# Expert rows loaded after the previous buffer's last reader, 64-bit weights turned in two parts, GpSimd's subtractions cut into pieces

## The chip, the cores and the metric

The kernel runs on one core of a Trainium2 chip. A core has TensorE (PE in the profile; its weight loads are PEld), VectorE (DVE), ScalarE (ACT), GpSimd (POOL) and SyncE (SP, which here only starts transfers). The metric is the device time of one execution in microseconds (us). Three executions of the kernel before took 1007.85, 1008.3 and 1010.31 us; the median is 1008.3 us.

## The reference

Three stages follow each other: a recurrent attention (delta rule) over 4 batches, 8 heads and 768 steps; a mixture of 8 experts in which each of 3072 tokens goes to one expert; and a gated layer with matrices of 384x1536, 384x1536 and 1536x384. Of the last two:

```python
def _moe_ref(x, w_gate, w_output_gate, w1, w2):
    logits = x @ w_gate
    e_idx = np.argmax(logits, axis=1)
    ...                                     # gate_w: softmax weight; eom: sigmoid(x @ w_output_gate)
    for e in range(E):                      # 8 experts
        mask = e_idx == e
        h = np.maximum(x[mask] @ w1[e], 0.0)
        ye = h @ w2[e]
        out[mask] = gate_w[mask, None] * eom[mask, e, None] * ye

def _moe2_ref(x, w_gate, w_val, w_out):
    gate = 1.0 / (1.0 + np.exp(-(x @ w_gate)))
    return (gate * (x @ w_val) @ w_out).astype(np.float32)
```

The matrices of the gated layer are float64; the kernel gets their bits as pairs of 32-bit words.

## The kernel before

The program has one stretch for each stage. The attention fills the first 270 us, the experts lie at about 270 to 540 us, the gated layer at 540 to 1007 us. The change touches the expert stretch.

**Precision.** Each product of float32 matrices is made of three TensorE passes, of a high and a low half: `hi` is a rounded copy (ScalarE, `copy`), `lo = src - hi` a subtraction (VectorE or GpSimd).

**Jobs and blocks.** `Experts.run` goes through nine jobs: jobs 0 and 1 are the first expert in two parts of 256 tokens, jobs 2 to 8 the other experts in windows of 460, 436, 416, 404, 396, 388 and 380 tokens. The window is in every shape (`hl 128x436` is job 3), so rows can be placed by it. A job has four blocks `j`, a block two halves `f`. In a half TensorE makes nine products of layer 1 into a PSUM tile `h` (L992, two buffers); ScalarE makes `hh = relu(h)` (L995) and VectorE `hl = max(h,0) - hh` (L996); then come nine products of layer 2 of the half before, into three tiles `y` (L955), of which three read `hl`. In block 2, `x_prep` (L903) prepares the next job: ScalarE scales its rows `XR` (L885), TensorE turns them in three groups of four (L897) into the tiles `xp`, `XTP` and a tile `h`, which takes one turn of the two `h` buffers; ScalarE and VectorE make `xh` and `xl` of them (L900, L901).

**Rows.** `rows(k)` (L873) moves a job's token rows from DRAM into `XR` (two buffers). It stands at the start of block 1 of the job before (L980). When a job's last layer-2 products are done, four small products `nm` (L968) take the token numbers out of its `XR`, ScalarE copies them into the tile (L970), and SyncE writes them out (`perm`, L971): that is the buffer's last reader.

**Expert weights.** `load` (L908) moves `w1r` and `w2r` (two buffers each), `high` makes `w1h`, `w2h` on ScalarE (L928), `low` makes `w1l`, `w2l` in one instruction of 128x768 (L933), five of sixteen on VectorE, the others on GpSimd.

**64-bit weights.** While the experts run, `hook` turns 24 tiles (128x384) of the gated layer's matrices into float32: in the second half of block `q` (from the ninth block on) it starts the load of tile `q` into one of four buffers `XG` (L828) and calls `narrow` on tile `q - 1`, five VectorE instructions (L839 to L843; below n1 to n5) that work in `XG` and in one buffer `xt`. Then ScalarE makes the high half (`wgh` or `wvh`, L815) and GpSimd the low half (`wgl` or `wvl`, L816, one instruction of 128x384). The next tile's n1 writes `xt`, so it waits for GpSimd.

**Order.** A scheduler of the framework places each engine's instructions by a model of their times; the order of the code is its starting point. So the code says what depends on what, and the built program says what stands behind what: `nm`, for one, needs only the rows, and is put where the scheduler expects them to have landed, a job early. Each engine takes its instructions strictly in that order, SyncE's transfers too. Line L78 is a wrapper, under which the instructions of the first jobs appear.

Of the kernel before, what the change touches and what calls it, by code (L numbers as in the profile page):

```python
# [7 lines left out]
F32 = mybir.dt.float32  # L8
# [5 lines left out]
ALU = mybir.AluOpType  # L14
# [798 lines left out]
def split_hi_lo(nc, hi, lo, src, eng, act=None):  # L813

    (act or nc.scalar).copy(out=hi, in_=src)  # L815
    eng.tensor_tensor(out=lo, in0=src, in1=hi, op=ALU.subtract)  # L816
# [12 lines left out]
    return r.rearrange("p (a b t) -> p a b t", a=shape[0], t=2)  # L829


def narrow(nc, t, r):

    if r.dtype == F32:
        return r
    V = nc.vector
    u = t.bitcast(U32)
    lo, hi = r[..., 0], r[..., 1]
    V.tensor_scalar(out=u, in0=hi, scalar1=3, scalar2=0x3FFFFFFF, op0=ALU.logical_shift_left, op1=ALU.bitwise_and)  # L839
    V.scalar_tensor_tensor(out=u, in0=hi, scalar=0xC0000000, in1=u, op0=ALU.bitwise_and, op1=ALU.bitwise_or)  # L840
    V.tensor_scalar(out=hi, in0=u, scalar1=0xFF800000, scalar2=None, op0=ALU.bitwise_and)
    V.scalar_tensor_tensor(out=lo.bitcast(F32), in0=lo, scalar=2.0**-52, in1=hi.bitcast(F32), op0=ALU.mult, op1=ALU.mult)
    V.tensor_tensor(out=t, in0=lo.bitcast(F32), in1=t, op=ALU.add)  # L843
    return t


# [10 lines left out]
class Experts:  # L857
# [72 lines left out]

    def low(self, b, i, engine):
        h, l = self.W[b][i]
        engine.tensor_tensor(out=l, in0=self.raw[b][i], in1=h, op=ALU.subtract)  # L933

    def split(self, upto):
        while self.n_split < min(upto, len(self.blocks)):
# [8 lines left out]
    def run(self, y2T, pp, xp, hook=lambda q, f: None, first=False):  # L945
        sp, jobs = self.sp, self.jobs
        self.xp = [(pp, "xp", 1), (xp, "XTP", 1), (pp, "h", 2)]
        own, b, pend = {}, -1, None

        def layer2(p):  # L950
            k, f, w2, hh, hl, ys = p
            n = jobs[k].n
            for c in range(3):
                for i, (l, r) in enumerate(PASS):
                    self.T.matmul(out=ys[c][:, 0:n], lhsT=w2[l][:, f % 2, 128 * c : 128 * c + 128], rhs=(hh, hl)[r], start=(f == 0 and i == 0), stop=(f == 7 and i == 2), skip_group_check=True)  # L955
            if f == 7:
                off = jobs[k].off
                for c in range(3):
                    o = y2T[:, c, ds(off, n)]
                    if c == 1:  # L960
                        self.A.copy(out=o, in_=ys[c][:, 0:n])
                    else:
                        self.V.tensor_copy(out=o, in_=ys[c][:, 0:n])

                ps = xp.tile([128, 512], F32, tag="GL", name="nm", bufs=1)[0:1].rearrange("p (r q) -> p r q", r=4)[:, :, 0 : n // 4]
                XR = self.XR.pop(k)
                for r in range(4):
                    self.T.matmul(out=ps[:, r], lhsT=XR[0 : n // 4, r, 384:385], rhs=self.idt[0 : n // 4, 0 : n // 4], start=True, stop=True)  # L968
                row = XR[0:1].rearrange("p r c -> p (r c)")[:, 0:n]
                self.A.copy(out=row.rearrange("p (q r) -> p q r", r=4), in_=ps.rearrange("p r q -> p q r"))  # L970
                self.SP.dma_start(out=self.perm[ds(off, n)].rearrange("n o -> o n"), in_=row)  # L971

        for q in range(4 * len(jobs)):
            k, j = divmod(q, 4)
            job = jobs[k]
            n = job.n
            if j == 0:
                ys = [pp.tile([128, 512], F32, tag=f"y{c}", name=f"y{c}") for c in range(3)]
            if j == 1 and k + 1 < len(jobs) and not first:
                self.rows(k + 1)  # L980
            if not job.shares:
                b += 1
                own[j] = b
                if not first:
                    self.load(b + 3)
            w1, w2 = self.W[own[j]]
            xh, xl = self.X[k]
            for f in (2 * j, 2 * j + 1):
                hp = pp.tile([128, 512], F32, tag="h", name="h", bufs=2)
                for i, (l, r) in enumerate(PASS):  # L990
                    for c in range(3):
                        self.T.matmul(out=hp[:, 0:n], lhsT=w1[l][:, c, 128 * (f % 2) : 128 * (f % 2) + 128], rhs=(xh, xl)[r][:, c], start=(i == 0 and c == 0), stop=(i == 2 and c == 2))  # L992
                hh = sp.tile([128, WMAX], F32R, tag="hh", name="hh", bufs=2)[:, 0:n]
                hl = sp.tile([128, WMAX], F32R, tag="hl", name="hl", bufs=2)[:, 0:n]
                self.A.activation(out=hh, in_=hp[:, 0:n], func=AF.Relu)  # L995
                self.V.scalar_tensor_tensor(out=hl, in0=hp[:, 0:n], scalar=0.0, in1=hh, op0=ALU.max, op1=ALU.subtract)  # L996
                if f % 2 == 0 and not first:
                    self.split(b + 2)
                if pend:
                    layer2(pend)  # L1000
                pend = (k, f, w2, hh, hl, ys)
                hook(q, f % 2)
                first = first and q < 7
            if j == 2 and k + 1 < len(jobs) and not first:
                self.x_prep(k + 1, self.A)
        layer2(pend)


def kernel_body(tc, a, out):
    nc = tc.nc  # L1010
    V, A, G, T, SP = nc.vector, nc.scalar, nc.gpsimd, nc.tensor, nc.sync
    with ExitStack() as ctx:
# [11 lines left out]
        if True:  # L1024
# [13 lines left out]
            gs = ctx.enter_context(tc.tile_pool(name="gt_s", bufs=1, side="left"))  # L1038
            jobs = [Job(E0), Job(E1, row=E0, shares=True)] + [Job(n) for n in WINS]
# [40 lines left out]
            gv = [[yp.tile([128, 3, DF2], F32R, name=n + p) for p in "hl"] for n in ("wg", "wv")]  # L1080
# [44 lines left out]
            wide = {}  # L1125
# [1 line left out]
            keep = [t.rearrange("p c f -> p (c f)") for t in gv[1]]  # L1127
            E.keep = {2: keep[0], 3: keep[1]}
            E.n_split = 2
            queued, head = [], []  # L1130

            def first_high():

# [3 lines left out]
            def hook(q, f):  # L1137
                i = 2 * q + f
                if i == 0:
                    E.high(2)  # L1140
                    E.low(2, 0, E.G)
                    tail(1)
                elif i == 1:
                    tail(2)
                    tail(3)
                    E.low(2, 1, E.V)
                elif i == 2:
                    E.high(3)
                    E.low(3, 0, E.V)
                    E.low(3, 1, E.V)  # L1150
                    E.n_split = 4
                elif i == 3:
                    order()
                    E.rows(1)
                    E.load(6)
                if i == QX:
                    E.x_scale(1, (E.V, E.A))
                if i == QT:
                    for c in range(3):
                        E.x_turn(1, c)  # L1160
                if i in (10, 12):
                    E.split(E.n_split + 1)
                if i == 14:
                    queued.append(E.SP)
                    nc_ = tc.nc
                    E.use((nc_.vector, nc_.scalar, nc_.gpsimd, nc_.tensor, nc_.sync))
                if i == 10:
                    E.rows(2)
                if i == QS:
                    E.x_scale(2, (E.V,))  # L1170
                if i == 13:
                    for c in range(3):
                        E.x_turn(2, c)
                if i == SG:
                    A.activation(out=key[:, 0:1], in_=cst[0:1, 0:1], func=AF.Sigmoid)
                if i == YS:
                    head.extend(gs.tile([128, 2, ROW], F32, tag="XG", name="XG", bufs=4).rearrange("p a b -> p (a b)")[:, 0:512].bitcast(F32R) for _ in range(3))
                    first_high()
                if f == 0 or q < 8:
                    return  # L1180
                q -= 8
                if q < 24:
                    r = gs.tile([128, 2, ROW], F32, tag="XG", name="XG", bufs=4).rearrange("p a b -> p (a b)")
                    wide[q] = load_wide(queued[0] if q < 4 else SP, r, gv_src(q)[2], [3, 128])
                if 1 <= q < 25:
                    w, cols, _ = gv_src(q - 1)
                    f = narrow(nc, gs.tile([128, 3, 128], F32, tag="xt", name="xt", bufs=1), wide.pop(q - 1))
                    split_hi_lo(nc, *[t[:, :, cols] for t in gv[w]], f, G)

            with tc.tile_pool(name="ex_p", bufs=1, reuse_waits="tile", space=PSUM) as pp:  # L1190
                E.run(y2T, pp, gp, hook, True)
# [4 lines left out]
            with tc.If(placed < NTOK):  # L1196
                with tc.tile_pool(name="ov", bufs=1) as ov:
                    q = ov.tile([1, 2, 64 + NE * NW_], F32, name="ov_q")
                    tab = ov.tile([1, 4, NE * NW_], I32, name="ov_tab")
                    z = ov.tile([112, ROW], F32, name="ov_z")  # L1200
                    first = ov.tile([1, NE], F32, name="ov_first")
# [191 lines left out]
```

## Time and profile before

| | |
|---|---|
| median of three runs | 1008.3 us |
| profiled execution, its own time | 1008.28 us |
| span of its instructions | 1006.6 us |
| TensorE busy, whole span | 946.6 us (94%) |
| TensorE busy, 300 to 536 us (experts) | 223.98 of 236 us |
| TensorE busy, 545.5 to 975 us (gated layer) | 429.5 of 429.5 us |
| mean granted TensorE clock | 0.905 |

Times are counted from the first instruction of the span. A row of the timeline gives start, duration, engine, line, operation, and in brackets how long the engine sat idle before it and what it then waited for. A row of the waits gives the sum, the number of times and the longest. The granted clock is a share of 2.4 GHz: 1.00 is 2.4 GHz, 0.50 is 1.2 GHz.

### The profile page before, as it was taken

The page shows a single profiled execution, that of the slowest core. Times are in us where ns is not written, and L with a number is a line of the kernel's source. Part 1 is how long each engine was busy: PE and PEld are TensorE (multiplying, and loading weights), DVE is VectorE, ACT ScalarE, POOL GpSimd, SP SyncE. Part 2 cuts the span into 40 slices and gives each one's busy share as a digit, 9 for nine tenths or more (in the row PEclk, how much of TensorE's full clock was granted, in tenths as well). Part 3 has the DMA queues.
Part 4 walks back from the last instruction along what each step waited for, and adds up shares of the span by engine and source line. Part 5 has one row for each costly group of instructions (what it writes and reads, how often), then busy time and mean ns, then how long its engine had stood idle before and what let it go on. Part 6 is the DMA issues. An engine that isn't in the chain of part 4 may idle for free. (4 is left out here: it accounts for less than half of the span.)

```text
span 1006.6 us, 24686 instructions
## 1 busy us (share of the span) xinstructions
PE 946.6 (94%) x10261; PEld 834.2 (83%) x10262; DVE 494.0 (49%) x1379; ACT 368.7 (37%) x723; POOL 346.1 (34%) x439
## 2 busy tenths in 40 slices
PE   6888879899999989989999999999999999999996
PEld 6677768778898879889897888888888888888885
DVE  6999897984458776777534644113113112111111
ACT  2654546566445444445452222112112112111111
POOL 4363254442313444345340334222222222222322
PEclk7776687675599999989999999999999999999999
DMA  5878652234346445645422220000000000000000
GB/s 123 154 226 188 143 131 57 72 94 128 102 133 204 142 144 169 200 128 151 130 85 49 63 63 27 21 1 9 24 1 9 24 1 8 24 1 8 23 1 33
DMA packets 62871, 82.90 MB, mean 82 GB/s; under 512 B 10313, under 2 KB 55634, under 8 KB 62754
## 3 DMA queue, kind: packets, MB, share of 16 engines
q1 hardware_dynamic: 59042, 70.49, 26.2%
q0 software_dynamic: 3712, 10.78, 3.1%
q8 instruction: 82, 1.34, 0.6%
q14 instruction: 35, 0.29, 0.1%
HBM read 64.13 MB, written 15.80 MB: 79 GB/s over the span
## 5 line engine op out<-in xcount | busy, mean ns | idle before, releaser
L1314 DVE TENSOR_TENSOR gf<-gf,g 128x512 f32<-128x512 f32 x72 | 49.5, 688 | 312.7 <-PE g L1306 310.2
L816 POOL TENSOR_TENSOR gsl<-gf,gsh 128x512 fp32r<-128x512 f32 x68 | 89.3, 1314 | 273.6 <-ACT gsh L815 273.6
L1313 ACT ACTIVATE gf<-g 128x512 f32<-128x512 f32 x72 | 43.0, 597 | 191.2 <-PE g L1306 191.2
L815 ACT CAST gsh<-gf 128x512 fp32r<-128x512 f32 x69 | 42.8, 620 | 145.0 <-DVE gf L1314 143.0
L1280 PE MATMUL o<-wol,gsh 128*128 128x384 f32 x272 | 87.1, 339 | 0.0
L1280 PE MATMUL o<-woh,gsl 128*128 128x384 f32 x272 | 86.6, 336 | 0.0
L78 DVE TENSOR_TENSOR tmp<-X,Lt 128x96 f32<-128x96 f32 (+40 forms) x301 | 72.4, 271 | 1.6
L78 DVE TENSOR_TENSOR X<-X,tmp 128x96 f32<-128x96 f32 (+40 forms) x301 | 71.5, 268 | 1.0
L78 PE MATMUL GY<-KQ 48*64 48x128 f32 (+1 forms) x640 | 46.3, 405 | 20.6 <-DMA KQ<-in_st_dram 13.8
L996 DVE SCALAR_TENSOR_TENSOR hl<-h,hh 128x460 fp32r<-128x460 f32 (+7 forms) x57 | 33.1, 581 | 64.2 <-ACT hh L995 63.9
L1306 PE MATMUL g<-yl,wgh 128*128 128x512 f32 x216 | 62.5, 394 | 0.0
L1306 PE MATMUL g<-yl,wvh 128*128 128x512 f32 x216 | 62.4, 395 | 0.0
L1280 PE MATMUL o<-woh,gsh 128*128 128x384 f32 x272 | 62.2, 339 | 0.0
L955 PE MATMUL y<-hh,w2h 128*128 128x460 f32 (+6 forms) x168 | 60.8, 362 | 1.3 <-ACT hh L995 1.2
L1306 PE MATMUL g<-yh,wgh 128*128 128x512 f32 x180 | 60.7, 394 | 0.0
L955 PE MATMUL y<-hh,w2l 128*128 128x460 f32 (+6 forms) x168 | 58.5, 348 | 0.0
L78 PEld LDWEIGHTS GY<-KQ 48*64 48x64 f32 x640 | 35.6, 205 | 26.1 <-issue 13.0
L1280 PEld LDWEIGHTS o<-woh,gsh 128*128 128x128 f32 x272 | 49.7, 188 | 6.2
L1280 PEld LDWEIGHTS o<-wol,gsh 128*128 128x128 f32 x272 | 50.6, 188 | 2.4
L933 POOL TENSOR_TENSOR w1l<-w1r,w1h 128x768 fp32r<-128x768 f32 x19 | 37.1, 1953 | 44.2 <-ACT w1h L928 44.0
L1306 PE MATMUL g<-yh,wgl 128*128 128x512 f32 x180 | 51.8, 394 | 0.0
L1306 PE MATMUL g<-yh,wvh 128*128 128x512 f32 x180 | 51.6, 394 | 0.0
(325 smaller groups left out, 2228.3 us busy)
## 6 DMA issues: line engine op xcount, KB each, us to landing
w1r<-in_w_dram SPq DMA_DIRECT2D x32, 384.0 KB
w2r<-in_w_dram SPq DMA_DIRECT2D x32, 384.0 KB
KQ<-in_st_dram SPq DMA_DIRECT2D x40, 192.0 KB
disp<-zrow SPq DMA_DIRECT2D x8, 772.0 KB
VT<-in_vtok_dram SPq DMA_DIRECT2D x96, 48.0 KB
kt<-in_ktok_dram SPq DMA_DIRECT2D x96, 48.0 KB
XG<-in_m2g_dram SPq DMA_DIRECT2D x12, 384.0 KB
XG<-in_m2v_dram SPq DMA_DIRECT2D x12, 384.0 KB
```

Source lines behind the costliest of these rows:

```text
L78: r = f(*args, **kw)
L815: (act or nc.scalar).copy(out=hi, in_=src)
L816: eng.tensor_tensor(out=lo, in0=src, in1=hi, op=ALU.subtract)
L933: engine.tensor_tensor(out=l, in0=self.raw[b][i], in1=h, op=ALU.subtract)
L955: self.T.matmul(out=ys[c][:, 0:n], lhsT=w2[l][:, f % 2, 128 * c : 128 * c + 128], rhs=(hh, hl)[r], start=(f == 0 and i == 0), stop=(f == 7 ...
L996: self.V.scalar_tensor_tensor(out=hl, in0=hp[:, 0:n], scalar=0.0, in1=hh, op0=ALU.max, op1=ALU.subtract)
L1280: T.matmul(out=ops_[m][:, 0:384], lhsT=gh[l][:, 128 * m : 128 * m + 128], rhs=wo[r][:, f], start=(f == 0 and i == 0), stop=(f == 11 and i ...
L1306: T.matmul(out=ps, lhsT=gv[w][l][:, c, 128 * f : 128 * f + 128], rhs=Y[r][c], start=(i == 0 and c == 0), stop=(i == 2 and c == 2))
L1313: A.activation(out=gf, in_=gps[0], func=AF.Sigmoid)
L1314: V.tensor_tensor(out=gf, in0=gf, in1=gps[1], op=ALU.mult)
```

## The change

Three edits. `rows(k + 2)` is issued right behind the `perm` transfer of job `k` instead of at block 1 of job `k + 1`. `narrow` is cut behind its third instruction: n1 to n3 are issued in a block's first half, n4, n5, the high copy and the subtraction in its second, so that an `hl` lies between. GpSimd's subtractions are issued in pieces: three of 128x256 for `w1l`, two of 128x384 for `w2l`, three of 128x128 for `wgl` and `wvl`; those of VectorE stay whole.

```diff
     def low(self, b, i, engine):
         h, l = self.W[b][i]
-        engine.tensor_tensor(out=l, in0=self.raw[b][i], in1=h, op=ALU.subtract)
+        r = self.raw[b][i]
+        if engine is self.G:
+            for k in range(r.shape[1]):
+                engine.tensor_tensor(out=l[:, k], in0=r[:, k], in1=h[:, k], op=ALU.subtract)
+        else:
+            engine.tensor_tensor(out=l, in0=r, in1=h, op=ALU.subtract)
...
                 self.SP.dma_start(out=self.perm[ds(off, n)].rearrange("n o -> o n"), in_=row)
+                if 0 < k < len(jobs) - 2:
+                    self.rows(k + 2)
...
-            if j == 1 and k + 1 < len(jobs) and not first:
-                self.rows(k + 1)
...
-                if f == 0 or q < 8:
+                if q < 8:
                     return
                 q -= 8
+                if f == 0:
+                    if 1 <= q < 25:
+                        turn.append(narrow_ops(nc, gs.tile([128, 3, 128], F32, tag="xt", name="xt", bufs=1), wide.pop(q - 1)))
+                        for op in turn[0][1][:3]:
+                            op()
+                    return
...
                     w, cols, _ = gv_src(q - 1)
-                    f = narrow(nc, gs.tile([128, 3, 128], F32, tag="xt", name="xt", bufs=1), wide.pop(q - 1))
-                    split_hi_lo(nc, *[t[:, :, cols] for t in gv[w]], f, G)
+                    f, ops = turn.pop()
+                    for op in ops[3:]:
+                        op()
+                    hi, lo = [t[:, :, cols] for t in gv[w]]
+                    A.copy(out=hi, in_=f)
+                    for c in range(3):
+                        G.tensor_tensor(out=lo[:, c], in0=f[:, c], in1=hi[:, c], op=ALU.subtract)
```

`narrow_ops` returns the five instructions of `narrow` as a list; `narrow` itself, used in the gated layer, runs them one after the other as before.

The scheduler makes its own order of this. On VectorE, around the third turn of job 3's rows (`xl<-h,xh 128x436`) in job 2; n1 is `xt<-XG` (TENSOR_SCALAR), n2 `xt<-XG,xt` (SCALAR_TENSOR_TENSOR), n3 `XG<-xt`, n4 `XG<-XG`, n5 `xt<-XG,xt` (TENSOR_TENSOR). Before:

```order
L996 SCALAR_TENSOR_TENSOR hl<-h,hh 128x460
L841 TENSOR_SCALAR XG<-xt 128x384
L842 SCALAR_TENSOR_TENSOR XG<-XG 128x384
L1119 TENSOR_LOAD tab
L843 TENSOR_TENSOR xt<-XG,xt 128x384
L901 TENSOR_TENSOR xl<-h,xh 128x436
L839 TENSOR_SCALAR xt<-XG 128x384
L840 SCALAR_TENSOR_TENSOR xt<-XG,xt 128x384
L996 SCALAR_TENSOR_TENSOR hl<-h,hh 128x460
```

Now:

```order
L1010 SCALAR_TENSOR_TENSOR hl<-h,hh 128x460
L844 TENSOR_TENSOR xt<-XG,xt 128x384
L1133 TENSOR_LOAD tab
L910 TENSOR_TENSOR xl<-h,xh 128x436
L840 TENSOR_SCALAR xt<-XG 128x384
L841 SCALAR_TENSOR_TENSOR xt<-XG,xt 128x384
L1010 SCALAR_TENSOR_TENSOR hl<-h,hh 128x460
```

n3 and n4 of the earlier tile have moved in front of the first `hl`; n1 and n2 of the next still stand in front of the second.

On SyncE, around the start of job 3 (window 436): from the `perm` transfer of that job, which the scheduler has put early, to the load of job 4's rows (`XR<-disp 112x1544`), which go into the buffer of job 2. Before:

```order
L971 DMA perm<-XR 1x436
L828 DMA XG<-in_m2v_dram 128x3x256
L916 ISA
L916 DMA w1r<-in_w_dram 128x3x256
L828 DMA XG<-in_m2g_dram 128x3x256
L917 ISA
L917 DMA w2r<-in_w_dram 128x2x384
L1116 TENSOR_LOAD tab
L876 ISA
L876 DMA XR<-disp 112x1544
```

Now:

```order
L985 DMA perm<-XR 1x436
L925 ISA
L925 DMA w1r<-in_w_dram 128x3x256
L828 DMA XG<-in_m2v_dram 128x3x256
L926 ISA
L926 DMA w2r<-in_w_dram 128x2x384
L1130 TENSOR_LOAD tab
L885 ISA
L885 DMA XR<-disp 112x1544
```

One `XG` load less stands in this piece; the rows still stand behind a `w1r`, an `XG` and a `w2r` load.

On ScalarE, in job 6 (window 396) just ahead of the copy of the token numbers `XR<-nm 1x388`. Before:

```order
L928 CAST w2h<-w2r 128x768
L815 CAST wvh<-xt 128x3x128
L995 ACTIVATE hh<-h 128x396
L928 CAST w1h<-w1r 128x768
L970 COPY XR<-nm 1x388
```

Now:

```order
L1009 ACTIVATE hh<-h 128x396
L909 CAST xh<-XTP 128x388
L937 CAST w2h<-w2r 128x768
L1009 ACTIVATE hh<-h 128x396
L937 CAST w1h<-w1r 128x768
L984 COPY XR<-nm 1x388
```

The high copy `wvh` no longer stands between `w2h` and this `hh`.

## Rows read from the trace of the kernel before

**Rows 1.** Windows: length, busy us (count) of each engine, PEclk, DMA, GB/s.

```profile
300.00:536.00 236.00, 223.98 (x1243) 207.43 (x1241) 151.99 (x238) 111.36 (x204) 99.90 (x62) 0.98 0.49 147
378.20:381.60 3.40, 3.40 (x11) 3.09 (x11) 2.15 (x5) 0.62 (x2) 0.38 (x1) 0.51 0.94 313
443.10:449.90 6.80, 5.78 (x17) 5.68 (x18) 3.68 (x8) 2.61 (x5) 1.00 (x1) 0.50 0.53 176
545.50:975.00 429.50, 429.50 (x2039) 373.14 (x2038) 99.51 (x163) 94.57 (x161) 121.04 (x100) 1.00 0.06 19
```

**Rows 2.** Waits of TensorE, 300 to 536 us: sum, times, longest.

```profile
PE h L992 <- DVE hl L996: 4.8, 2, 2.9
PE nm L968 <- DMA XR<-disp: 3.1, 2, 1.7
PE y L955 <- ACT hh L995: 1.2, 2, 1.0
PE y L955 <- DVE hl L996: 0.9, 2, 0.7
PE h L992 <- DVE xl L901: 0.8, 1, 0.8
PE h L78 <- DVE hl L78: 0.7, 1, 0.7
```

**Rows 3.** Timeline of TensorE: the three longest waits of the stretch.

```profile
358.05 0.34 PE L968 MATMUL nm<-cst,XR 104*1 104x104 f32 x2 [1.70 <-DMA XR<-disp]
...
377.52 0.66 PE L992 MATMUL h<-xh,w1h 128*128 128x436 f32 x2 [1.92 <-DVE hl L996]
...
444.12 1.38 PE L992 MATMUL h<-xh,w1h 128*128 128x404 f32 x3 [2.92 <-DVE hl L996]
```

**Rows 4.** Timeline, VectorE and ScalarE before the stall at 377 us.

```profile
371.24 0.36 DVE L839 TENSOR_SCALAR xt<-XG 128x384 uint32<-128x384 uint32 x1
...
372.38 0.54 ACT L995 ACTIVATE hh<-h 128x436 fp32r<-128x436 f32 x1 [0.97 <-PE h L992]
...
376.86 0.60 DVE L996 SCALAR_TENSOR_TENSOR hl<-h,hh 128x436 fp32r<-128x436 f32 x1
```

**Rows 5.** Timeline, VectorE and GpSimd before the stall at 444 us.

```profile
438.09 1.99 POOL L933 TENSOR_TENSOR w2l<-w2r,w2h 128x768 fp32r<-128x768 f32 x1
...
438.42 2.08 DVE L840 SCALAR_TENSOR_TENSOR xt<-XG,xt 128x384 uint32<-128x384 uint32 x1
...
440.04 2.13 POOL L933 TENSOR_TENSOR w1l<-w1r,w1h 128x768 fp32r<-128x768 f32 x1
...
440.53 1.86 DVE L841 TENSOR_SCALAR XG<-xt 128x384 uint32<-128x384 uint32 x1
...
443.50 0.57 DVE L996 SCALAR_TENSOR_TENSOR hl<-h,hh 128x404 fp32r<-128x404 f32 x1
```

**Rows 6.** Line 816, GpSimd and others: ns min/median/max, starts.

```profile
L816 POOL TENSOR_TENSOR wgl<-xt,wgh x12: 1009/1020/1664, 311.7 to 481.7; 128x384 fp32r<-128x384 f32 x12
```

**Rows 7.** Line 933, the same columns.

```profile
L933 POOL TENSOR_TENSOR w1l<-w1r,w1h x19: 1822/1852/2292, 332.0 to 525.3; 128x768 fp32r<-128x768 f32 x19
```

**Rows 8.** Timeline, VectorE and GpSimd before the wait at 347 us.

```profile
344.74 1.85 POOL L933 TENSOR_TENSOR w2l<-w2r,w2h 128x768 fp32r<-128x768 f32 x1 [0.37 <-ACT w2h L928]
344.80 2.21 DVE L840 SCALAR_TENSOR_TENSOR xt<-XG,xt 128x384 uint32<-128x384 uint32 x1
...
346.94 0.62 DVE L996 SCALAR_TENSOR_TENSOR hl<-h,hh 128x460 fp32r<-128x460 f32 x1
```

**Rows 9.** Timeline, VectorE's n5 and SyncE's transfers from 348 us.

```profile
348.46 0.56 DVE L843 TENSOR_TENSOR xt<-XG,xt 128x384 f32<-128x384 f32 x1
...
349.05 0.37 SPq L828 DMA_DIRECT2D XG<-in_m2g_dram  x1
...
350.82 0.34 SPq L876 DMA_DIRECT2D XR<-disp  x1
```

**Rows 10.** Timeline, VectorE before the wait at 311 us.

```profile
309.01 2.06 DVE L843 TENSOR_TENSOR xt<-XG,xt 128x384 f32<-128x384 f32 x1
```

More of the change, by code (lines that the diff above doesn't have):

```diff
@@ L829, in load_wide, with narrow_ops @@
     return r.rearrange("p (a b t) -> p a b t", a=shape[0], t=2)
-def narrow(nc, t, r):
+def narrow_ops(nc, t, r):
     if r.dtype == F32:
-        return r
+        return r, []
     V = nc.vector
@@ L838, in narrow @@
     lo, hi = r[..., 0], r[..., 1]
[L839 to L843, printed above, removed]
+    return t, [
+        lambda: V.tensor_scalar(out=u, in0=hi, scalar1=3, scalar2=0x3FFFFFFF, op0=ALU.logical_shift_left, op1=ALU.bitwise_and),
+        lambda: V.scalar_tensor_tensor(out=u, in0=hi, scalar=0xC0000000, in1=u, op0=ALU.bitwise_and, op1=ALU.bitwise_or),
+        lambda: V.tensor_scalar(out=hi, in0=u, scalar1=0xFF800000, scalar2=None, op0=ALU.bitwise_and),
+        lambda: V.scalar_tensor_tensor(out=lo.bitcast(F32), in0=lo, scalar=2.0**-52, in1=hi.bitcast(F32), op0=ALU.mult, op1=ALU.mult),
+        lambda: V.tensor_tensor(out=t, in0=lo.bitcast(F32), in1=t, op=ALU.add),
+    ]
+def narrow(nc, t, r):
+    t, ops = narrow_ops(nc, t, r)
+    for f in ops:
+        f()
     return t
@@ L1129, in kernel_body @@
             E.n_split = 2
-            queued, head = [], []
+            queued, head, turn = [], [], []
             def first_high():
```

## The prediction

> **What bounds the kernel now.** I read the busy time by stretch first. In the gated layer TensorE works without a gap (429.50 of 429.50 us from 545.5 us), at a granted clock of 1.00; the attention is untouched by the edits. In the expert stretch, 300 to 536 us, TensorE is busy 223.98 of 236 us, so 12.0 us are idle, and two pieces of 3.4 and 6.8 us run at 0.50 of the clock, 1.2 GHz, in which half the time is lost: 5.1 us [rows 1]. Nothing else is to be had: 17.1 us at most. What TensorE gains here reaches the end one for one, because it is the only busy engine behind it.
>
> The waits of TensorE, read next, say who holds it up: twice VectorE's `hl`, from which a PSUM buffer `h` becomes free (4.8 us, the longer 2.9); twice the landing of the next job's rows, at `nm` (3.1, longer 1.7); and five small waits on `hh`, `hl` and `xl` [rows 2]. The timeline places the long ones: rows at 358 us (1.70), `hl` at 377 (1.92) and at 444 (2.92) [rows 3]. The waits at 377 and at 444 are the two with a half-rate piece behind them (378.2 and 443.1 us), the second the longer; behind the 1.70 there is none.
>
> Why is `hl` late? At 377 its input `hh` was ready at 372.92 and `hl` began at 376.86: it stood behind n1 to n5 [rows 4]. An n3 needs 0.36 us like the n1 in that group, an n5 0.56 [rows 4, 9]. Beside GpSimd's subtractions they take about 2: at 438 us n2 took 2.08 and n3 1.86, and each ended 0.4 and 0.2 us after a GpSimd instruction [rows 5]. So VectorE's work between SBUF buffers and GpSimd's exclude each other for a whole instruction. `hl` reads PSUM and kept its 0.6 us everywhere. The two also take turns: GpSimd's second subtraction stood right behind its first (438.09 + 1.99 = 440.08), yet n2 got in between, GpSimd waited for it (2.13 instead of 1.85), and then n3 lost again [rows 5, 7].
>
> **GpSimd's pieces.** 384 elements take 1.02 us and 768 take 1.85 [rows 6, 7], so an instruction costs 0.19 us plus 2.17 ns an element: a piece of 256 is 0.74 us, of 128 0.47. `w1l` becomes 2.2 us (+0.4), `w2l` 2.0 (+0.2), the low half of a turned tile 1.4 (+0.4). GpSimd is busy 99.9 of the 236 us and has room [rows 1]; the +0.4 delays the next tile's n1, which waits for it.
>
> What a piece saves depends on how many of VectorE's instructions meet GpSimd ahead of an `hl`.
> - One meets it: at 344.80 n2 waited for a whole `w2l` and `hl` began at 346.94 [rows 8]. With pieces the first ends at 345.76, n2 0.4 later, and `hl` begins at 346.1, 0.8 earlier: the wait of 0.7 on it goes [rows 2]. −0.7.
> - At 309 us n5 met `w2l`, and an n3 had met `w1l` before it [rows 10]. A `w1l` in pieces holds n3 to n5 for three pieces of 0.74 and the `w2l` comes too late for them. The 0.7 on `hl` at L78 goes too. −0.7.
> - At 377 and at 444 all of n2 to n5 stand ahead of `hl`, in the built order after the change as before it. At 444, step by step with the overlaps of [rows 5]: piece of `w2l` to 439.11, n2 to 439.53, piece to 440.38, n3 to 440.60, piece of `w1l` to 441.17, n4 to 441.59, piece to 442.16, n5 to 442.58. Two lost turns of 1.85 have become four of 0.74 to 1.02, so `hl` comes at 442.5 instead of 443.50: 1.0 earlier. If n1 comes 0.4 later and loses a turn itself, 0.2 earlier. I take 0.6 at either place: −1.2, bounds 0 and −4.8.
>
> The Trainium skill has a rule that would give more: in "SBUF — State Buffer", section "Who interferes with whom", the instruction that issues second is blocked until the first has finished, and no more is said. Read so, VectorE would wait for one piece, once, and the long waits would be gone; the trace agrees on the lock (2.08 us for an n2) and adds that the next instruction loses again.
>
> **The turned weights.** The built order changes less than the code: the scheduler had already put `hl` between n-instructions. Three places gain. On ScalarE the `hh` in job 6 no longer stands behind the copy of a turned tile: the longer wait on `hh`, 1.0 us, goes. −1.0. The `xl` that cost 0.8 has n4 and n5 ahead of it instead of n1 to n3, of which one met GpSimd: −0.5, bounds 0 and −0.8 [rows 2]. And n3, n4 come ahead of an `hl` in job 2, so that n5 is earlier.
>
> **The rows.** Their transfer is not much earlier in the built order: one `XG` load less ahead of it in job 2, and still one with a wait. In the trace that load waited for n5 (348.46 + 0.56 = 349.02), went out at 349.05, the rows' transfer at 350.82 [rows 9], and they landed by 358.05. So the landing follows that n5, and it is the lock that moves it: with n2 0.8 earlier and n3 to n5 held by one piece, n5 ends 0.8 to 1.5 earlier. `nm` itself has moved back by three products in jobs 3 and 5, some 0.6 us (an estimate; two products show 0.66 with their overlap [rows 3]). In job 3 TensorE comes to `nm` at 356.35 − 0.7 + 0.6 = 356.25, the rows at 358.05 − 1.2 = 356.85: the wait falls from 1.7 to 0.6, −1.1. In job 5 1.4 falls to 0.1, −1.3. Together −2.4, bounds 0 (the same n5 holds it) and −3.1.
>
> **The clock.** If the wait at 377 is 1.3, it is shorter than the 1.70 that had no half-rate piece behind it; at 2.3 the one at 444 lies between those with 3.4 and with 6.8 us. I count one piece of 3.4 us less, half of it: −1.7, bounds 0 and −5.1.
>
> **What is given back.** Rows of the order in jobs 6 and 7 get n-instructions that stood elsewhere, every tile is turned 0.4 us slower, and ScalarE's copies of `nm` and `xh` stand behind others. The trace has no price for these; nearest are the small waits of 0.7 to 1.0 [rows 2]. I take two and a half of 0.7, +1.8, bounds 0 and +5.
>
> **Sum.** −0.7 − 0.7 − 1.2 − 1.0 − 0.5 − 2.4 − 1.7 + 1.8 = −6.4. The profiled execution took 1008.28 us (span 1006.6 and 1.7 around it), the median of three is 1008.3: 1001.9 us.
>
> **Rivals.**
> 1. *Slower: the turns.* VectorE loses a turn to every piece. With the low half of a tile 0.4 later, GpSimd's `w2l` gets ahead of n1, and ahead of one `hl` stand five lost turns instead of two. The place is the third turn of the rows in each job, where a `h` buffer hangs on `hl` directly (377 and 444 us). If the next narrowing is late there by 1 us or more, job 3's wait is 3.0 with 6.8 us at half rate (+1.1 + 1.7), job 5's the same +0.4, and job 4 gets what job 3 has now (1.9 + 1.7). With −1.4 from 309 and 345 us: +5.4, 1013.7 us. For it: n3 lost again right after n2 [rows 5]. Against it: the walk above, in which four short turns are less than two long ones. It decides once n1 meets a piece itself. Chance 0.12.
> 2. *No change: the waits move.* The long `hl` rows are unchanged in the order, the rows hang on the same n5, the clock falls as before; only 309, 345 us and the `hh` gain (−2.4), and new small waits give +1.8 back: 1007.7 us. For it speaks how little the order changes. Chance 0.25.
> 3. *One lost turn only.* If VectorE loses to one piece and then gets ahead, both long waits go (−4.8) with both half-rate pieces (−5.1), and the rest as above without what is given back (−5.3): −15.2, 993.1 us. Against it stands [rows 5]. This is what the rule of the Trainium skill by itself would make of it. Chance 0.13.
>
> **How the numbers follow.** The forecast has 0.50; its own range, by the bounds of the clock and of what is given back, is 997.5 to 1005. Runs of this kernel can tell 0.3%, 3 us, from no change. Faster by more: forecast and rival 3, 0.63. Within: rival 2, 0.25. Slower: rival 1, 0.12. Leaving out the far half of rival 3 and most of rival 1, the range for 8 in 10 is 995 to 1009.5.
>
> **What would show it.** n-instructions of about 1.2 us at most instead of 2; GpSimd's pieces at 0.74 and 0.47; no wait on `hl` near 311 and 347 us; `nm` waiting under 0.7; the waits on `hl` in jobs 3 and 5 (436 and 404) still there, at 1.3 and 2.3, with at most one half-rate piece of 3.4 us between 370 and 450 us. I am wrong if those two waits are gone or longer than before, or if waits on `hl`, `hh` or `xl` of over 1 us stand where there are none now.

## The result and the profile after

The changed kernel takes 998.47 us (median of four runs, 996.54 to 1000.42), the kernel before 1008.92 us (four runs, 1007.85 to 1010.31): a ratio of 0.988, 95% interval 0.985 to 0.991. Forecast were 1001.9 us and a range of 995 to 1009.5, so the time lies 3.4 us below the forecast, inside its range. The profiled execution took 996.54 us, with a span of 994.8 us against 1006.6 before.

First the place of the difference. Windows of the kernel after (columns as in [rows 1]): the whole expert stretch, from the first layer-1 product to the first product of the gated layer; the part of it that answers to [rows 1]; and the gated layer.

```profile
274.96:528.93 253.97, 248.57 (x1492) 234.34 (x1493) 159.83 (x299) 125.04 (x232) 132.31 (x179) 0.98 0.50 149
300.00:525.80 225.80, 223.45 (x1291) 210.30 (x1290) 144.34 (x241) 113.86 (x208) 124.59 (x169) 1.00 0.52 155
545.50:975.00 429.50, 429.50 (x2042) 373.37 (x2041) 92.62 (x151) 93.96 (x160) 119.73 (x99) 1.00 0.05 18
```

The same whole stretch of the kernel before:

```profile
271.44:541.96 270.52, 256.05 (x1493) 238.01 (x1493) 168.92 (x299) 123.90 (x232) 107.34 (x70) 0.97 0.47 140
```

The stretch is 16.5 us shorter with the same 299 instructions on VectorE, which is busy 9.1 us less, and with 109 instructions more on GpSimd, which is busy 25 us more. From 300 us to its end (the second line) TensorE is idle 2.35 us where it was 12.0, and no piece runs at half rate (1.00 against the 0.98 of [rows 1]). The rest of the program is longer by 4.7 us in this pair of executions: the attention, which no edit touches, by 3.5, and the gated layer, whose clock is taken up in the last section, by 1.2. So the span falls by 11.8.

Waits of TensorE in the kernel after, 290 to 540 us, where [rows 2] had six lines (the first one here is the entry into the gated layer, which is outside [rows 2]):

```profile
PE g L1331 <- PEq L1221: 3.0, 1, 3.0
PE h L1006 <- DVE hl L1010: 1.9, 2, 1.2
PE nm L982 <- DMA XR<-disp: 0.4, 1, 0.4
```

The two waits on `hl` are the ones forecast to stay, in jobs 3 and 5. They are 1.17 and 0.76 us where [rows 3] had 1.92 and 2.92; the 1.70 on the rows is gone. TensorE in the kernel after, the two places:

```profile
376.50 0.87 PE L1006 MATMUL h<-xh,w1h 128*128 128x436 f32 x3 [1.17 <-DVE hl L1010]
...
437.21 0.82 PE L1006 MATMUL h<-xh,w1h 128*128 128x404 f32 x3 [0.76 <-DVE hl L1010]
```

Timeline of VectorE and GpSimd in the kernel after, before the first of them (it answers to [rows 4]; a GpSimd row joins the pieces of one subtraction, as x2 and x3):

```profile
371.16 0.36 DVE L840 TENSOR_SCALAR xt<-XG 128x384 uint32<-128x384 uint32 x1 [0.34 <-POOL wvl L1213]
371.18 2.51 POOL L945 TENSOR_TENSOR w2l<-w2r,w2h 128x384 fp32r<-128x384 f32 x2
371.55 1.26 DVE L841 SCALAR_TENSOR_TENSOR xt<-XG,xt 128x384 uint32<-128x384 uint32 x1
372.85 1.06 DVE L842 TENSOR_SCALAR XG<-xt 128x384 uint32<-128x384 uint32 x1
373.65 2.86 POOL L945 TENSOR_TENSOR w1l<-w1r,w1h 128x256 fp32r<-128x256 f32 x3
373.94 0.97 DVE L843 SCALAR_TENSOR_TENSOR XG<-XG 128x384 f32<-128x384 uint32 x1
374.95 0.97 DVE L844 TENSOR_TENSOR xt<-XG,xt 128x384 f32<-128x384 f32 x1
375.84 0.60 DVE L1010 SCALAR_TENSOR_TENSOR hl<-h,hh 128x436 fp32r<-128x436 f32 x1
```

Each of n2 to n5 loses one turn, to a piece: 1.26, 1.06, 0.97, 0.97 us. GpSimd pays too: its five pieces take 5.37 us here, where the unblocked lengths add up to 4.3. Still n1 to n5 take 4.8 us from the start of the first to the end of the last, where it was 5.7. The lines of n2, n3 and GpSimd's pieces over the whole kernel (minimum, median, maximum in ns):

```profile
L841 DVE SCALAR_TENSOR_TENSOR xt<-XG,xt x24: 544/559/1266, 309.6 to 486.1; 128x384 uint32<-128x384 uint32 x24
L842 DVE TENSOR_SCALAR XG<-xt x24: 351/362/1069, 310.2 to 487.6; 128x384 uint32<-128x384 uint32 x24
...
L945 POOL TENSOR_TENSOR w1l<-w1r,w1h x57: 722/742/1375, 334.2 to 513.1; 128x256 fp32r<-128x256 f32 x57
L945 POOL TENSOR_TENSOR w2l<-w2r,w2h x32: 1000/1148/1436, 331.8 to 510.7; 128x384 fp32r<-128x384 f32 x32
```

A lost turn costs n2 0.7 us instead of the 1.5 of [rows 5]. The `w1l` piece takes 0.74 us, as worked out from [rows 6, 7].

### The profile page after: what moved, and what is told of

The parts are those of the page before. It is cut to its first block, busy times and chain, and to the rows that moved or that the text cites. A ratio compares the mean times of both kernels' runs of the same rounds, so it can differ in the third digit from the quotient of the medians.

```text
span 994.8 us, 24800 instructions
## 1 busy us (share of the span) xinstructions
PE 943.7 (95%) x10261; PEld 833.7 (84%) x10262; DVE 484.5 (49%) x1379; ACT 370.4 (37%) x723; POOL 374.5 (38%) x548
## 5 line engine op out<-in xcount | busy, mean ns | idle before, releaser
L945 POOL TENSOR_TENSOR w1l<-w1r,w1h 128x256 fp32r<-128x256 f32 x57 | 47.5, 860 | 32.5 <-ACT w1h L937 32.5
```

Source lines behind the costliest of these rows:

```text
L945: engine.tensor_tensor(out=l[:, k], in0=r[:, k], in1=h[:, k], op=ALU.subtract)
```

## The experiments

All ratios are to the kernel before on the same chip, with 95% intervals. "Stretch" is the expert stretch of the profiled execution, measured as above; "n time" is the sum of the 120 instructions n1 to n5 of the 24 tiles, which is 57 us where nothing blocks them; "half rate" lists the lengths in us of the pieces at a granted clock of 0.50 from 300 us on, without the one that some kernels have at the entry into the gated layer.

| kernel | ratio | stretch | n time | `hl` waits of `h` | half rate |
|---|---|---|---|---|---|
| before | 1 | 270.5 | 86.6 | 1.92, 2.92 | 3.4, 6.8 |
| after | 0.988 (0.985 to 0.991) | 254.0 | 77.2 | 1.17, 0.76 | none |
| e1 pieces only | 0.986 (0.981 to 0.991) | 256.0 | 77.0 | 1.21, 0.76 | none |
| e2 rows and two parts | 1.000 (0.997 to 1.003) | 265.2 | 86.4 | 1.93, 2.90 | none |
| e3 whole, order of after | 0.9985 (0.996 to 1.001) | 267.1 | 91.6 | 3.13, 3.07 | 3.4, 6.8 |
| e4 finer pieces | 0.987 (0.983 to 0.992) | 255.4 | 70.6 | 0.45, 0.88 | none |
| e5 weights' pieces | 0.988 (0.983 to 0.993) | 258.4 | 78.0 | 2.37 | 3.4 |
| e6 tiles' pieces | 0.995 (0.991 to 0.998) | 262.3 | 91.3 | 3.8 in all | 3.4 |
| e7 weights on VectorE | 0.986 (0.981 to 0.990) | 249.4 | 57.1 | none | none |
| e8 changed kernel again | 0.985 (0.982 to 0.989) | 255.8 | 77.7 | 1.19, 0.76 | none |
| e9 as e7, more runs | 0.984 (0.981 to 0.988) | 252.2 | 57.0 | none | none |
| e10 before, weights on VectorE | 0.986 (0.982 to 0.990) | 252.7 | 57.0 | none | none |

**Which edit does it (e1 to e3).** e1 has the pieces alone:

```diff
...
+        if engine is self.G:
+            for k in range(r.shape[1]):
+                engine.tensor_tensor(out=l[:, k], in0=r[:, k], in1=h[:, k], op=ALU.subtract)
...
-                    split_hi_lo(nc, *[t[:, :, cols] for t in gv[w]], f, G)
...
+                    A.copy(out=hi, in_=f)
+                    for c in range(3):
+                        G.tensor_tensor(out=lo[:, c], in0=f[:, c], in1=hi[:, c], op=ALU.subtract)
```

> The kernel before with GpSimd's subtractions in pieces and neither of the other two edits. Its instructions stand in the changed kernel's order on every engine. Theory L (the pieces alone) and theory O (the order that the scheduler makes when it sees pieces): both 998 us, ratio 0.988. Theory P (the moved rows and the two parts of the turning each have a share): over 1002 us.

e2 has the two other edits and whole subtractions:

```diff
-            if j == 1 and k + 1 < len(jobs) and not first:
-                self.rows(k + 1)
...
+                if 0 < k < len(jobs) - 2:
+                    self.rows(k + 2)
...
+                    f, ops = turn.pop()
+                    for op in ops[3:]:
+                        op()
                     split_hi_lo(nc, *[t[:, :, cols] for t in gv[w]], f, G)
```

> The rows' load moved and the turning in two parts, no pieces. The built order is that of the kernel before on every engine. Theories L and O: 1008.5 us, ratio 1.000 within 0.003. Theory P: 3 to 6 us faster than before.

e3 keeps the subtractions whole and adds behind each some of two elements, so that the scheduler sees as many instructions as in the changed kernel and builds very nearly the same order. The small ones write values that are there already:

```diff
         engine.tensor_tensor(out=l, in0=self.raw[b][i], in1=h, op=ALU.subtract)
+        if engine is self.G:
+            for k in range(1, self.raw[b][i].shape[1]):
+                engine.tensor_tensor(out=l[:, k, 0:2], in0=self.raw[b][i][:, k, 0:2], in1=h[:, k, 0:2], op=ALU.subtract)
...
```

> Whole subtractions on GpSimd, each followed by subtractions of 2 elements that write the same values again, as many as there are further pieces. The scheduler then makes the changed kernel's order (TensorE and ScalarE the same, VectorE but for one place, SyncE but for two). Theory L (VectorE waits for shorter instructions): the n-instructions take up to 2 us again, waits on hl of 2 us at windows 436 and 404 come back, with half-rate pieces: 1005 to 1009 us. Theory O (the order): 998 to 1000 us, no long waits.

The pieces alone give 989.28 us against 1003.29, as much as all three edits. The two code moves together give none, and the reason is in the build: with them the scheduler puts out the instructions of the kernel before, in the same order on every engine. With the pieces alone it puts out the order of the changed kernel. Every move of an instruction that the rows of the order under "The change" show was therefore the scheduler's answer to the pieces. e2's waits of TensorE (282 to 528 us) are those of [rows 2] but for the rows' landing:

```profile
PE h L1001 <- DVE hl L1005: 4.8, 2, 2.9
PE nm L977 <- DMA XR<-disp: 2.2, 2, 1.2
PE y L964 <- ACT hh L1004: 1.2, 2, 1.0
```

e3 separates the order from the length. Its waits of TensorE in the same stretch:

```profile
PE h L995 <- DVE hl L999: 6.2, 2, 3.1
PE nm L971 <- DMA XR<-disp: 1.1, 2, 0.7
PE y L958 <- DVE hl L999: 1.0, 1, 1.0
PE h L78 <- DVE hl L78: 0.7, 1, 0.7
```

The order alone removes the waits on `hh` and `xl` and shortens those on the rows, makes the two `hl` waits longer by 1.4 us and adds one of 1.0 in job 4: no gain is shown, 0.9985 (0.996 to 1.001). So the gain hangs on the length of GpSimd's instructions. The pieces in the order of the kernel before were not run; how much of the gain needs the new order beside them stays open. The half-rate pieces are there again, behind the two long waits:

```profile
375.50:378.90 3.40, 3.40 (x11) 3.10 (x10) 2.05 (x5) 1.22 (x2) 0.51 (x4) 0.50 0.90 295
440.30:447.10 6.80, 6.12 (x18) 6.04 (x19) 4.25 (x9) 2.61 (x5) 1.61 (x5) 0.50 0.54 176
```

**Which pieces, and how fine (e4 to e6).** e4 halves the pieces of the experts' weights:

```diff
+            n = r.shape[2] // 2
             for k in range(r.shape[1]):
-                engine.tensor_tensor(out=l[:, k], in0=r[:, k], in1=h[:, k], op=ALU.subtract)
+                for s in (slice(0, n), slice(n, 2 * n)):
+                    engine.tensor_tensor(out=l[:, k, s], in0=r[:, k, s], in1=h[:, k, s], op=ALU.subtract)
```

> The changed kernel with w1l in six pieces of 128x128 and w2l in four of 128x192. Theory L: n-instructions beside w1l and w2l take 0.8 to 1.0 us at most, the waits of 1.17 and 0.76 us at windows 436 and 404 shrink to under 0.6, 997 to 999 us (little is left to gain). Rival (the turns: a lost turn for every piece, so more pieces cost more): hl comes later than in the changed kernel, waits over 1.2 us, 1001 us or more. The order changes too, which blurs it.

e5 has, of e1's two hunks, only the first (`w1l`, `w2l`), e6 only the second (`wgl`, `wvl`).

> The kernel before with pieces for w1l and w2l alone; wgl and wvl stay one instruction of 128x384. Theory L: the long lost turns are those beside w1l and w2l, so nearly all of the gain stays: ratio 0.986 to 0.991, waits on hl at windows 436 and 404 of 0.7 to 1.3 us. Rival (the turned tiles' low half, released earlier piece by piece, matters): ratio over 0.994.

> Pieces for wgl and wvl alone; w1l and w2l stay whole. Theory L: n-instructions still up to 2 us, waits on hl of 2 to 3 us, ratio 0.996 to 1.003. Rival as in the run before: ratio under 0.992.

e4's n2 line, which answers to the L841 line above:

```profile
L841 DVE SCALAR_TENSOR_TENSOR xt<-XG,xt x24: 541/558/983, 305.4 to 484.3; 128x384 uint32<-128x384 uint32 x24
```

More turns at half the length cost no more: n time falls by another 6.6 us, and GpSimd's is up by 20 us over the stretch with nobody waiting for it. The total does not show it (990.56 us beside e1's 989.28), since only some 2 us of waits were left. Of the two waits that were to shrink to under 0.6 us one did (0.45); the other is 0.88. The weights' pieces alone bring the gain (0.988, overlapping e1's interval), but not as expected in the trace: one wait on `hl` is gone and the other, at window 404, is 2.37 us instead of 0.7 to 1.3. e6 missed its expectation: the tiles' pieces leave n time above that of before, 91.3 us, and still gain 0.2 to 0.9%. That n time does not fall has a reason in the program: n1 waits for the earlier tile's subtraction, so n1 to n5 never lie beside one. Its order is another again, and its profile has one half-rate piece where before has two; the cause of that half per cent was not separated.

**The lock taken away (e7 to e10).** In e7 VectorE makes every `w1l` and `w2l`, so that GpSimd has none of them:

```diff
-                self.low(b, i, self.V if self.nw % 16 in DV else self.G)
+                self.low(b, i, self.V)
...
-                    E.low(2, 0, E.G)
+                    E.low(2, 0, E.V)
```

> The changed kernel with every w1l and w2l made on VectorE (0.95 us each, whole), so that GpSimd has only the turned tiles' pieces and nothing long is left to wait for. Theory L: every n-instruction under 1 us; VectorE's busy time rises by about 35 x 0.95 = 33 us of 236 (152 to 185), and what its load costs is seen apart from the lock: the waits on hl at windows 436 and 404 under 0.8 us. If load on VectorE counted for more than the lock, waits on hl grow and the ratio is over 0.99; else 0.985 to 0.988.

e8 is the changed kernel, e9 is e7, and e10 has e7's diff on the kernel before, without any of the three edits; all on one chip.

> The changed kernel once more, as the measure for the next two on the same chip: ratio 0.985 to 0.990.

> The kernel of e7. Its expert stretch was 249.4 us against 254.0 of the changed kernel, so by theory L it should be some 4 us faster than e8: ratio to before lower than that of e8 by 0.003 to 0.005. If VectorE's load costs elsewhere (the start of the gated layer), equal to e8.

> The kernel before with one thing changed: w1l and w2l all on VectorE; wgl and wvl whole on GpSimd (1.02 us). Theory L: what is left to wait for is 1.02 us at most, so nearly as e9, waits on hl under 0.7 us, ratio within 0.003 of e9. Rival (pieces matter for another reason than their length): ratio over 0.99.

n2 in e10, all 24 of them:

```profile
L840 DVE SCALAR_TENSOR_TENSOR xt<-XG,xt x24: 542/551/565, 308.7 to 464.5; 128x384 uint32<-128x384 uint32 x24
```

Its slowest takes 565 ns. A whole `w1l`, now on VectorE, in the same kernel:

```profile
L933 DVE TENSOR_TENSOR w1l<-w1r,w1h x26: 941/951/960, 327.0 to 509.3; 128x768 fp32r<-128x768 f32 x26
```

The n-instructions take 57.0 us together, so none is blocked any more, where the kernel before has an n2 of up to 2.2 us. This is the most direct evidence for the lock: neither instruction nor data of n2 changed, and what went is GpSimd's work beside it. (The tiles' subtractions stay on GpSimd, but n1 waits for them.) VectorE takes 0.95 us for a subtraction that costs GpSimd 1.85 [rows 7]. e10's whole stretch:

```profile
273.64:526.30 252.66, 247.66 (x1493) 235.55 (x1493) 172.02 (x338) 124.64 (x232) 36.31 (x31) 0.98 0.49 150
```

39 instructions have gone from GpSimd (70 to 31) to VectorE (299 to 338), at 0.95 us some 37 us of work, and VectorE's busy time is up by only 3.1 (168.92 to 172.02). Most of the work came back as n time, which is 29.6 lower; the two do not add up exactly, since busy time counts instructions that overlap once. The 33 us that were expected of e7 did not come either: VectorE is busy 172.85 us in its stretch, 13.0 more than in that of after.

The stretches of e9 and e10 are 3.6 and 3.2 us shorter than that of e8, but the medians are 989.31 (e8), 988.42 (e9) and 990.25 (e10) with overlapping intervals: the three cannot be told apart, and no version is shown to beat the changed kernel. e9 was expected 0.003 to 0.005 below e8 and came 0.001 below it; in the profiles the attention took 3.6 us more in e9, and the gated layer 463.1 us in both, so the load on VectorE cost nothing there. Two changed lines (e10) do as well as the three edits.

## Why the prediction was right, step by step

**The mechanism held.** GpSimd and VectorE's work between SBUF buffers exclude each other for a whole instruction, and VectorE loses again at each next instruction. The walk of four short turns instead of two long ones is what the timeline shows, also in job 5 (1.27, 1.06, 0.98, 0.97 us for n2 to n5). The sign came out, and that the two `hl` waits stay; the longest n-instruction is 1.36 us (n4) where about 1.2 was told.

**Its terms, by the rows of after and of the runs.**

- `hl` in job 2 (−0.7) and at 311 us (−0.7): both waits are gone. At 311 us it came as told: n3 to n5 stand beside the three pieces of `w1l` (0.73, 0.98 and 0.98 us). At 347 us the number is luck. n2 was to lose one short turn, and it meets no piece at all, because ScalarE makes `w2h` behind the `hh` there now: GpSimd's `w2l` starts at 347.26 us, after the `hl` at 346.32. e3, with whole subtractions in this order, has no wait there either: this 0.7 belongs to the order.
- `hl` in jobs 3 and 5 (−0.6 each): −0.75 and −2.16. From n1 to the late `hl` it took 5.62 and 5.48 us and takes 4.68 and 4.70, so the turns give 0.9 and 0.8, near the forecast's 0.6 and the walk's 1.0. The rest of job 5's was not in the sum, and is shown below.
- The rows (−2.4): 3.1 us have become 0.4, −2.7. In other executions of the same order 1.3 (e8) and, in e1, 2.1 us were left, and e2, with the order of the kernel before, has 2.2 instead of 3.1, so the size of this term is that of one pair. Its cause is in doubt too: the lock was to move the landing, and e3, with whole subtractions, has 1.1.
- `hh` (−1.0) and `xl` (−0.5): −1.2 and −0.8, both lines gone.
- The clock (−1.7): −5.1, the upper bound. Both half-rate pieces went, one was counted. The reason that was given, a wait shorter than one without such a piece, does not hold in other runs (the last section), so this term was a guess.
- Given back (+1.8): nothing. The waits of after have no line that [rows 2] lacks; only the one at the entry into the gated layer, outside [rows 2], grew from 2.45 to 3.05. The step that failed is this one, together with the clock: the sum took 0.1 us for the two (−1.7 + 1.8), and they brought −5.1.

The rest of job 5's wait comes from the tile before. VectorE, ScalarE and GpSimd in the kernel before, ahead of [rows 5], put together from the timelines of the three engines:

```profile
432.80 2.00 DVE L841 TENSOR_SCALAR XG<-xt 128x384 uint32<-128x384 uint32 x1
...
435.78 0.56 DVE L843 TENSOR_TENSOR xt<-XG,xt 128x384 f32<-128x384 f32 x1
...
437.32 0.58 DVE L996 SCALAR_TENSOR_TENSOR hl<-h,hh 128x404 fp32r<-128x404 f32 x1 [0.99 <-ACT hh L995]
...
436.37 0.51 ACT L815 CAST wgh<-xt 128x384 fp32r<-128x384 f32 x1 [4.10 <-DVE xt L843]
436.79 0.50 ACT L995 ACTIVATE hh<-h 128x404 fp32r<-128x404 f32 x1
...
436.96 1.02 POOL L816 TENSOR_TENSOR wgl<-xt,wgh 128x384 fp32r<-128x384 f32 x1 [2.39 <-ACT wgh L815]
...
438.02 0.36 DVE L839 TENSOR_SCALAR xt<-XG 128x384 uint32<-128x384 uint32 x1
```

The same place in the kernel after:

```profile
427.02 0.90 DVE L842 TENSOR_SCALAR XG<-xt 128x384 uint32<-128x384 uint32 x1
...
429.33 0.60 DVE L844 TENSOR_TENSOR xt<-XG,xt 128x384 f32<-128x384 f32 x1
...
430.93 0.58 DVE L1010 SCALAR_TENSOR_TENSOR hl<-h,hh 128x404 fp32r<-128x404 f32 x1 [0.99 <-ACT hh L1009]
...
429.97 0.52 ACT L1211 CAST wvh<-xt 128x384 fp32r<-128x384 f32 x1 [2.79 <-DVE xt L844]
430.39 0.50 ACT L1009 ACTIVATE hh<-h 128x404 fp32r<-128x404 f32 x1
...
430.56 1.29 POOL L1213 TENSOR_TENSOR wvl<-xt,wvh 128x128 fp32r<-128x128 f32 x3 [1.04 <-ACT wvh L1211]
...
431.89 0.36 DVE L840 TENSOR_SCALAR xt<-XG 128x384 uint32<-128x384 uint32 x1 [0.39 <-POOL wvl L1213]
```

In both, a blocked n3 delays n5, n5 the high copy on ScalarE, the copy GpSimd's low half, and the low half the next n1, which writes `xt`: one chain through three engines. (The `hl` ahead of n1 ends sooner, at 437.90 and 431.51.) TensorE wanted the buffer at 441.20 in the kernel before (444.12 − 2.92) and at 436.45 after (437.21 − 0.76). Counted back from there, n1 began 3.18 us ahead before and 4.56 after, 1.4 earlier. The n3 took 2.00 us in the one and 0.90 in the other, 1.1 less, and began 1.0 earlier by the same count (8.40 and 9.43 us ahead), for a reason that was not traced; of these 2.1 us, 0.4 went to the instructions between n3 and n5, where an `xl` stands now, and 0.3 to the way from n5 to n1, where the low half in pieces takes longer. I had walked only the turns between n1 and the `hl`, not those of the tile before.

The terms as measured add up to −0.7 − 0.7 − 2.9 − 2.7 − 1.2 − 0.8 − 5.1 = −14.1 of the stretch's −16.5. The other 2.4 lie in TensorE's busy time, which fell by 7.5 us (256.05 to 248.57) where the clock explains 5.1; why was not traced. Of the span's −11.8, 4.7 were lost in stages that the edits don't touch. In the later runs the ratio of 0.985 to 0.986 (e1, e8) is 14 us. So the forecast was 3.4 us off as a time, but its −6.4 is 8 us short of the gain in those runs and 10 us short of that of the stretch here. That the time lies inside the range is luck in part: e8's ratio would have put it at 993.3 us (of 1008.3), below 995.

**What was wrong in the argument.** The part "The turned weights" read its gains off the built order as those of the turning in two parts. e1 and e2 show that the two code edits move nothing: the pieces made the scheduler choose that order. And the order's own terms (`hh`, `xl`, `nm`) are not shown to be worth anything by themselves (e3, 0.9985): without the shorter pieces about half of the waits that it takes away (2.4 of 4.9 us) come back as `hl` waits, which the sum did not allow for. Two small slips: the short waits of [rows 2] are six, not five, and the bounds of the clock and of what is given back make 996.7 to 1006.8 us of the sum, not 997.5 to 1005.

**The rivals.** The slower one was to decide once n1 meets a piece itself. In the changed kernel it never does (n1 takes 364 ns at most); in e4 and e5 it does (up to 744 and 925 ns), and they gain as much. e4, with twice as many pieces, has even 6.6 us less n time. "No change" describes the code moves without the pieces (e2) and the order alone (e3). One lost turn only, 993.1 us, comes near the gain of e1 and e8, and both half-rate pieces are gone; its reason is wrong, since in jobs 3 and 5 each of n2 to n5 lost a turn (the timeline above), and both long waits stayed, if shorter. The rule in the Trainium skill, "SBUF — State Buffer", section "Who interferes with whom", that the pair of ports is held for a whole instruction and that the other engine is fully blocked, agrees with the trace: n2 1.26 us beside a piece of 1.0 to 1.2, and 0.55 in e10. That one lost turn would be all is not in the rows.

## What to carry to other kernels

Work on GpSimd that nobody waits for can still be on the critical path, if VectorE's work between SBUF buffers runs beside it: compare the maximum of a VectorE line with its minimum (2214 against 547 ns here), and either cut GpSimd's instruction to the length of VectorE's own, or give it to VectorE. Where a scheduler orders the program, look at what it builds from each edit alone before a gain is credited to it: two of three edits here were built into the program that was there before. And a better order without the shorter instruction only moved the wait.

## What the runs showed of the hardware that was not expected

**The same wait does not always bring the clock down.** In the kernel before, half rate followed waits of 1.92 and 2.92 us, and in e3 waits of over 3 us. In e2, with the same order as before and the same waits of 1.93 (at 370.75 us) and 2.90 us (at 435.51), the clock stayed: this is its window behind the first, which answers to the second line of [rows 1].

```profile
371.43:374.83 3.40, 3.40 (x19) 3.22 (x19) 3.14 (x7) 1.45 (x3) 0.37 (x1) 1.00 0.97 332
```

TensorE does 19 instructions there where it did 11. In e5 and e6 no half rate follows the waits of 2.37 and 2.46 us on `hl`; their one piece each (at 485.4 and 425.6 us) stands behind small products of `nm` and `xp`, with waits of 0.32 and 1.14 us. At the entry into the gated layer all twelve profiles have a wait of 2.4 to 3.1 us; behind it six show no half rate (e1, e5, e6, e8 to e10), four 3.4 us of it (before, e3, e4, e7) and two 6.8 (after, e2), and the rest of the program takes 463.1, 464.4 to 464.7 and 465.8 to 465.9 us. That is the 1.2 us by which the gated layer is longer in after than in before. What decides it stays open.

So the −5.1 us belong to this pair of profiles. The stretches of e2 and e1, on one chip, have no half-rate piece behind a wait on `hl`:

```profile
265.11:530.33 265.22, 251.50 (x1493) 234.28 (x1493) 168.47 (x299) 123.77 (x232) 107.62 (x70) 0.98 0.47 143
268.44:524.47 256.03, 249.08 (x1493) 234.69 (x1493) 159.71 (x299) 125.07 (x232) 132.29 (x179) 0.98 0.49 148
```

In that pair the pieces, with the order that the scheduler makes of them, are worth 9.2 us without the clock. The medians are 13.0 us apart (1002.32 and 989.28). How much of the gain over many executions is clock was not measured.

**The two engines alternate.** Beside a stream of GpSimd pieces VectorE gets in after each one and GpSimd after each of VectorE's, so the piece's length sets the price of a turn: 1.5 us on top of an n2 at 768 elements, 0.7 at 256 to 384, at most 0.43 (983 − 558 ns) in e4 at 128 to 192.

**The attention's length varies without an edit.** No edit touches it, and on one chip the experts begin at 265.1 to 270.1 us (e1 to e4), on another at 273.8 to 278.7 (e5 to e7). The same kernel has 275.0 (after) and 269.8 (e8) in two executions. Differences of 3 us between versions have to be read in the stretch, and need many runs to show in the total.
